# A fused transformer block on one core: fewer pair additions in five units, one transpose moved to TensorE, a new order, and the re-run test ahead of the last transfers

## The chip, the cores and the metric

The kernel runs on one core of one Trainium2 chip. The metric is device time in microseconds (us), the median of the runs of one kernel. The core's engines run side by side, each with its own instruction stream: TensorE (PE in the profile, its weight loads PEld), VectorE (DVE), ScalarE (ACT), GpSimd (POOL) and SyncE (SP), which in this kernel issues nearly all DMA transfers. Semaphores tie the streams together.

## The reference, cut to what matters

A transformer block over 2048 tokens of width 1024, with an attention half and a gated feed-forward half. Both halves are modulated by a vector `c`:

```python
sa, ca, ga, sb, cb, gb = split(silu(c) @ w_mod)
h = layernorm(x) * (1 + ca) + sa
q, k, v = h @ wq (32 heads of 32), h @ wk, h @ wv      # one k and one v for all heads
p = softmax(q k^T / sqrt(32));  x = x + ga * ((p v) @ wo)
h = layernorm(x) * (1 + cb) + sb
x = x + gb * ((silu(h @ w1) * (h @ w3)) @ w2)          # inner width 3584
```

Inputs and the output are bfloat16, the output 2048 x 1024.

## The kernel before, in words

Tokens are taken in 8 blocks of 256. For each block there are 8 attention units of 4 heads, so 64 units in all (`u`; block `u // 8`). A unit goes through the 2048 keys in 8 chunks, so there are 512 chunks. A chunk is eight score matmuls of 32 rows (`S<-QT,KT`, four side by side in the array), two exponentials on ACT (`U<-S`, 128x1024 each) into one of ten slots of `U`, and eight matmuls of the probabilities with V (`PB<-U,V`). The scores lie in six PSUM banks (`S` in the rows); two more (`PB`) serve everything else, and after the last chunk the six are used for that too.

The softmax denominators are made on two engines. VectorE adds the two key halves of two chunks at a time (`pairs`: `PS<-U`, 128x2048), then folds the eight results of a unit together with additions of 128x1024 (`PS<-PS`), and TensorE multiplies what is left with ones (`dens`: `PB<-PS,ONES`, four matmuls of 32 columns for each slot left). How far VectorE folds is `level(u)`: at 1 it doesn't fold and eight slots go to TensorE, at 2 four additions leave four slots, at 4 seven additions leave one. Before, units 0 to 7 are folded to level 2 (units 0 and 1 in a form of their own) and all later ones to level 4.

After a block's eight units come, in `wo` (from L1371), its output projection (`WO<-QT` rows), the residual, the second norm's statistics and its normalised tile `XNB`; then the norm is transposed and modulated, and the feed-forward half follows: 14 slabs of the products with w1 and w3 (`slab`; a tanh on ACT and two multiplications on VectorE each), and four quarters of the product with w2 (`quarter`, whose w2 slices come into `W2S`, and for the last block also into the memory of `QT` and `U`). The feed-forward half of a block is spread between the score chunks of the next block. What belongs to the last block runs after the last chunk.

The transpose of the second norm has two forms. Blocks 1 to 6 use two DMA transposes from `XNB` into the memory of the block before in `QT`, and eight modulations `QT<-QT,MODC` on VectorE. Blocks 0 and 7 use sixteen TensorE transposes (`IDENT,XNB`) into two PSUM banks, and VectorE modulates straight out of PSUM.

The program is recorded as a graph of operations (`Graph.op`). A table of numbers, `ORDER`, gives the sequence in which a small planner (`Placer`) commits them; that alone sets the order on each engine. A `b` behind a number picks the operation's other engine (`alts`): for the first norm's tiles and their copies ACT or VectorE, for the scaling of the first two columns of wq (`WO<-W,MODC`) VectorE or POOL. Where the planner's own clock sees TensorE idle for over 0.7 us in the middle of the run, `keep_on` puts in multiplications of the identity, `PB<-IDENT`, whose results are not used; `keep_warm` does so in the start (`S<-IDENT`).

The exponentials are taken without subtracting a maximum. A test at the end (`verdict`) writes a flag `AGAIN`; only if it is set does each engine run a second, guarded version of the whole program, which stands behind the first one in its stream. So each engine, at the end of its stream, waits for the flag, loads it (`TENSOR_LOAD`), and branches over the guarded program:

```python
for fn in self.ops[name]:
    fn(eng)
eng.wait_ge(sem[flag.sem], flag.val)
again = eng.value_load(tile)
with eng.If(again != 0):
    ... second.ops[name] ...
```

SyncE then waits for every output transfer, and a barrier of all engines ends the program. In the profile all recorded operations have line 22; the flag's load is L747, the branch L748, SyncE's waits L756, and the end of the block with its drains L758.

Of the kernel before, what the change touches and what calls it, by code (L numbers as in the profile page):

```python
# [119 lines left out]
7 1 11 0 4 2 5 8 3 6 16 12 9 13 10 17 18 60 22 15 19 59 20 27 14 21 28 412 29 37 30 31 23 24 26 32 36 77 33 38 61 39  # L120
69 40 34 102 41 25 62 35 68 63 42 70 103 64 71 65b 72 104 111 43 73 105 45 44 112 106 66 113 122 74 114 132 115 123
67 116 75 107 124 131 125 76 126 46 133 117b 47 127 108 134 128b 118 135 48 49 119 109 136 50 78 137 110b 129 79 80
130 162 99 81 82 163 85 58b 57 53 54 97 55 86b 52b 51 164 172 83 98b 56b 171 138 84 173 165 182 87 166 139 88 183 89
90 167 91 174 168 92 143 93 175 94 95 142 120 176 96 144 151 460 145 121b 140 146 152 461 169 153 147 141 462 154
148b 463 155 170b 464 149 156 184 192 242 185 150 186 177b 157b 465 187 466 243 421 191 158 467 178 193 159b 194 195
179 203 469 160 188b 196 470 197b 180 161 468 202 198 181 471 472 199b 189 473 204 211 100 205 206 190b 474 475 101
207 212 200 476 213 208b 222 214 223 201b 244 215 224 225 477 245 209 216 226 246 478 210 227 217b 228 229 247 230
480 232 248 233 234 231 235 479 249 218 236 250 252 219 251 481 253 487 254 482 255 237-239 256 240 483 501 241 484
# [5 lines left out]
317 316 585 318 591 609 319 610 592 320 594 611 595 321 612 596 613 593 597-599 587 600 614 601 615 605 602 616 603  # L134
282 604 283 617 606 618 607 284 619 608 285 633 327 620 621 328 286 622 329 634 330 623 332 331 624 635 333 625 334
335 626 636 627 322 336 628 323 637 324 629 630 325 631 638 337 338 326 632 339 656 340 657 287 341 288 658 639 659
289 660 290 640 641 661 642 291 662 643 663 644-648 664 665 652 649 650 666 342 680 343 667 668 651 344 669 653 345
# [9 lines left out]
1182 453 794 407 456 795 820 1308 454 455 408 796 1309 457 826 829-831 822 832 1310 1311 827 833 834 1312 835 836  # L147
409 840 1313 824 1314 410 828 1315 837 889 411 838 888 1316 1317 839 930 458 910 841 1318 842 909 844 843 846 847
931 1319 1320 845 459 848 1321 849 1332 851 1322 1323 850 852 1324 853 1334 854 1325 1326 855 867 1327 868 857 869
856 1328 870 858 1329 1337 859 862 1331 860 863 864 871 1330 865 861 1343 866 1357 1344 1358 873 1345-1347 872 1348  # L150
# [260 lines left out]
class Placer:  # L411

    SWITCH = {"F": 0.095, "S": 0.11, "A": 0.106, "C": 0.106}
    LAT = {("dve", "pe"): 0.12, ("act", "pe"): 0.1, ("act", "dve"): 0.06}
    SEM = 0.06
    SPAN = 8
    COLS = 12
    FULL = 36.0
    FETCH = 24.0
    GAP = 0.7  # L420

    def __init__(self, g, banks, later, plan, first=None, order=None):
        self.g = g
        self.plan = []
        off = {}
        for late, pes, sl, one, hold, change in plan:
# [312 lines left out]
    def emit_all(self, second, flag, tile, outs):  # L739
# [3 lines left out]
        def both(eng, name):  # L743
            for fn in self.ops[name]:
                fn(eng)
# [924 lines left out]
```

## Time and profile before

| | before |
|---|---|
| median of 3 runs | 1137.85 us (1137.28 to 1138.27) |
| profiled execution, its own time | 1138.92 us |
| its span, first to last instruction | 1137.1 us |
| PE busy | 1102.5 us (97%) |
| ACT busy | 1020.4 us (90%) |
| DVE busy | 993.3 us (87%) |
| POOL busy | 42.9 us (4%) |
| mean busy share of the DMA queue q1 | 66% |

The stages can be read from the views by their first and last instructions: the first exponential starts at 31.26 us, the last score chunk stands at 1031 us, and the last matmul ends at about 1131.7 us. A row of a group or of the timeline has start and length in us, then engine, line, operation, output and inputs by tile name without buffer numbers, shapes, and in brackets the idle time ahead of it and who ended it. PEclk in the windows is the granted TensorE clock as a share of full speed.

### The profile page before, as it was taken

Reading aid. Unit: us, or ns where it says so; the run is one execution under the profiler, and the core shown is the slowest. Engines: PE = TensorE matmul, PEld = TensorE weight load, DVE = VectorE, ACT = ScalarE, POOL = GpSimd, SP = SyncE. Lnnn points to the kernel's source line nnn. Section 1 sums busy time; section 2 is a strip of 40 time slices with the busy share of each in tenths; the row PEclk is TensorE's granted clock in tenths of the full one; section 3 lists DMA queues with packets and bytes.
Section 4 is the critical chain, followed back from the end, with each engine's and each line's share of the span. In section 5 each row is a group of like instructions: output and inputs, shape, how many; then the busy total and the mean of one; then the engine's idle time right before and its main releaser. Section 6 shows DMA issues by size and latency. Waiting matters only on the chain.

```text
span 1137.1 us, 37432 instructions
## 1 busy us (share of the span) xinstructions
PE 1102.5 (97%) x16864; PEld 755.2 (66%) x16891; DVE 993.3 (87%) x1634; ACT 1020.4 (90%) x1159; POOL 42.9 (4%) x93
## 2 busy tenths in 40 slices
PE   5999989999899999999999999999999999999998
PEld 5744546766467766777577766776667757777887
DVE  7998999999999989998999889998999899997441
ACT  5999999999999999999999999999999999993110
POOL 5300000000100000000000000000000000000000
PEclk9999999999999999999999999999999999999999
DMA  9321477675656676865696568768587558767983
GB/s 344 107 76 36 146 212 203 191 203 144 174 150 192 183 188 157 240 195 152 122 297 193 151 179 209 223 193 214 149 249 214 161 141 214 214 188 195 260 233 85
DMA packets 381544, 209.73 MB, mean 184 GB/s; under 512 B 17600, under 2 KB 373184, under 8 KB 381376
## 3 DMA queue, kind: packets, MB, share of 16 engines
q1 hardware_dynamic: 380944, 207.11, 66.0%
q8 instruction: 135, 2.21, 0.8%
q14 instruction: 33, 0.27, 0.1%
q10 hardware_dynamic: 432, 0.13, 0.1%
HBM read 199.89 MB, written 4.19 MB: 179 GB/s over the span
## 4 chain that ended last, share of the span: by engine, by line
PE 47%; ACT 41%; DVE 6%; DMA 2%; POOL 1%; issue 1%; SPq 1%; DVEq 0%
ACT U L22 38%; PE PB L22 34%; PE S L22 13%; ACT HT L22 3%; DVE PS L22 2%; DMA W<-in_A_wq_dram 1%; DVE ST L22 1%; DVE HT L22 1%; POOL RS L22 1%; SPq L22 1%; DMA HT<-in_B_w_dram 1%; DVE QT L22 1%; DMA W<-in_B_w_dram 0%; DVE X L22 0%; DVE XNB L22 0%
## 5 line engine op out<-in xcount | busy, mean ns | idle before, releaser
L22 ACT ACTIVATE U<-S 128x1024 bf16<-128x1024 f32 x1024 | 967.0, 1141 | 6.2 <-PE S L22 5.0
L22 DVE TENSOR_TENSOR PS<-U 128x2048 bf16<-128x2048 bf16 x256 | 308.8, 1213 | 9.6 <-ACT U L22 8.1
L22 DVE TENSOR_TENSOR PS<-PS 128x1024 bf16<-128x1024 bf16 (+1 forms) x420 | 284.5, 690 | 4.2
L22 PE MATMUL PB<-QT,W 128*128 128x256 bf16 (+1 forms) x2632 | 223.5, 273 | 0.1
L22 PE MATMUL S<-QT,KT 32*128 32x256 bf16 x4096 | 203.9, 273 | 7.9 <-ACT U L22 5.3
L22 PEld LDWEIGHTS PB<-QT,W 128*128 128x128 bf16 (+1 forms) x2632 | 167.4, 97 | 40.8 <-issue 22.2
L22 PE MATMUL PB<-W2S,HT 128*128 128x256 bf16 x1512 | 189.6, 273 | 0.0
L22 PEld LDWEIGHTS PB<-W2S,HT 128*128 128x128 bf16 x1512 | 137.1, 98 | 41.6 <-issue 22.6
L22 PEld LDWEIGHTS S<-QT,KT 32*128 32x128 bf16 x4096 | 60.8, 92 | 135.4 <-ACT U L22 121.8
L22 PE MATMUL PB<-U,V 128*32 128x256 bf16 x4032 | 126.9, 273 | 0.8 <-ACT U L22 0.8
L22 PE MATMUL PB<-QT,HT 128*128 128x256 bf16 (+1 forms) x1288 | 123.9, 273 | 0.9 <-DVE QT L22 0.6
L22 PEld LDWEIGHTS PB<-U,V 128*32 128x32 bf16 x4032 | 99.4, 96 | 23.2 <-issue 13.5
L22 ACT ACTIVATE HT<-PB 128x512 bf16<-128x512 f32 (+1 forms) x110 | 81.6, 741 | 32.0 <-PE PB L22 31.9
L22 PEld LDWEIGHTS PB<-QT,HT 128*128 128x128 bf16 (+1 forms) x1288 | 90.9, 97 | 23.2 <-issue 11.5
L22 PE MATMUL PB<-HT,W 128*32 128x512 bf16 (+2 forms) x884 | 97.8, 342 | 2.8 <-DVE HT L22 0.9
L22 DVE SCALAR_TENSOR_TENSOR HT<-HT,PB 128x512 bf16<-128x512 bf16 x103 | 70.4, 684 | 12.7 <-ACT HT L22 11.8
L22 PEld LDWEIGHTS PB<-HT,W 128*128 128x128 bf16 (+1 forms) x896 | 50.4, 97 | 33.2 <-issue 11.7
L22 DVE TENSOR_TENSOR HT<-HT,PB 128x512 bf16<-128x512 bf16 x98 | 66.7, 681 | 1.3 <-PE PB L22 0.6
L22 PE MATMUL PB<-WO,QT 128*128 128x512 bf16 (+1 forms) x266 | 54.8, 380 | 1.6 <-issue 1.3
L22 DVE STREAM_TRANSPOSE RB<-PB 128x256 f32<-128x256 f32 x63 | 28.1, 446 | 29.2 <-PE PB L22 28.7
L22 POOL TENSOR_SCALAR RS<-MV 128x1 f32<-128x1 f32 x32 | 13.4, 418 | 1001.0 <-DVE MV L22 994.8
L22 ACT ACTIVATE HT<-S 128x512 bf16<-128x512 f32 (+1 forms) x13 | 9.4, 728 | 36.7 <-PE S L22 36.7
(122 smaller groups left out, 674.8 us busy)
## 6 DMA issues: line engine op xcount, KB each, us to landing
W<-in_B_w_dram SPq DMA_DIRECT2D x150, 512.0 KB, 4.9
W2S<-in_B_w_dram SPq DMA_DIRECT2D x30, 1792.0 KB, 9.3
HT<-in_B_w_dram SPq DMA_DIRECT2D x74, 512.0 KB, 5.0
W2S<-in_w_mod_dram SPq DMA_DIRECT2D x8, 1024.0 KB, 5.7
X<-in_A_x_dram SPq DMA_DIRECT2D x8, 512.0 KB, 6.7
U<-in_w_mod_dram SPq DMA_DIRECT2D x4, 1024.0 KB, 11.6
out_dram<-X SPq DMA_DIRECT2D x7, 512.0 KB, 8.1
W2S<-in_A_x_dram SPq DMA_DIRECT2D x5, 512.0 KB, 11.1
```

Source lines behind the costliest of these rows:

```text
L22: return getattr(e, call[0])(*call[1], **call[2])
```

## The change

Four things change.

1. `level(u)` is 2 for units 13, 14, 15 and 17, and 1 for unit 16, which were all 4. That leaves out three additions in four units and seven in one, 19 of 128x1024, and adds 12 matmuls in four units and 28 in one, 76 of 32x256.
2. The second norm of block 1 takes TensorE's form of the transpose: two DMA transposes less, sixteen transposes of 128x128 more on TensorE; the eight modulations read PSUM.
3. `ORDER` is another sequence, from the first operation to the last.
4. In `both`, SyncE's last three operations and VectorE's last six are taken out of the main stream; the flag is tested ahead of them, and they are issued in both arms: ahead of the guarded program if the flag is set, and in a second `If` behind it otherwise. The other three engines keep their test at the end.

```diff
@@ ORDER (all lines differ; its first)
-7 1 11 0 4 2 5 8 3 6 16 12 9 13 10 17 18 60 22 15 19 59 20 27 14 21 28 412 29 37 30 31 23 24 26 32 36 77 33 38 61 39
+6 1 11 0 4 2 5 8 3 7 9 12 13 10 25 16-18 59 22 15 14 60 19 61 28 21 62 412 63 27 20 23 64 24 65 26 29 68 30 31 36 45
...
@@ class Placer
     GAP = 0.7
+    TAIL = {"sp": 3, "dve": 6}
...
         def both(eng, name):
-            for fn in self.ops[name]:
+            ops = self.ops[name]
+            cut = len(ops) - self.TAIL.get(name, 0)
+            for fn in ops[:cut]:
                 fn(eng)
             eng.wait_ge(sem[flag.sem], flag.val)
             again = eng.value_load(tile)
             with eng.If(again != 0):
+                for fn in ops[cut:]:
+                    fn(eng)
                 for s, v in last.items():
                     if v:
                         eng.wait_ge(sem[s], v)
                 for fn in second.ops[name]:
                     fn(eng)
+            if ops[cut:]:
+                with eng.If(again == 0):
+                    for fn in ops[cut:]:
+                        fn(eng)
             if name == "sp":
                 for n in outs:
                     eng.wait_ge(sem[n.sem], n.val)
...
         def level(u):
-            return 2 if u < 8 else 4
+            return {13: 2, 14: 2, 15: 2, 16: 1, 17: 2}.get(u, 2 if u < 8 else 4)
...
-                if 0 < n < NB - 1:
+                if 1 < n < NB - 1:
                     G.alias([("H2R", n, t)], h2k(n))
                     dma("sp", h2t(n)[:, :, t * P:(t + 1) * P], XN[t], ("H2", t), 1 << 18, reads=[("XN", t)],
                         writes=[("H2R", n, t)], vt=vt - 40, bw=100e3, transpose=True)
-            if 0 < n < NB - 1:
+            if 1 < n < NB - 1:
```

How the instructions stand is shown at three places. The first is the end of SyncE's stream. Before, the last output transfers, then the load of the flag and the branch; what stands behind the branch belongs to the guarded program:

```order
L22 DMA W2S<-in_B_w_dram 128x28x256
L22 DMA out_dram<-X 128x2x1024
L22 DMA out_dram<-X 128x2x256 x3
L22 DMA out_dram<-X 128x256 x2
L747 TENSOR_LOAD AGAIN
L748 COMPARE_AND_BRANCH
```

After, in the same place (the three rows behind the branch are those of the arm with the flag set, and stand once more behind the guarded program, after a second branch on line 760):

```order
L22 DMA W2S<-in_B_w_dram 128x28x256
L22 DMA out_dram<-X 128x2x1024
L22 DMA out_dram<-X 128x2x256 x2
L750 TENSOR_LOAD AGAIN
L751 COMPARE_AND_BRANCH
L22 DMA out_dram<-X 128x2x256
L22 DMA out_dram<-X 128x256 x2
```

Load and branch moved from behind the last transfer to between the transfers of the second and the third quarter. VectorE's stream has them in the corresponding place, ahead of its last three pairs of a multiplication and an addition.

The second place is TensorE around the second norm of block 1, from the end of that block's output projection (`WO<-QT`) to its first slab (`QT,HT` and `QT,W` are the norm times w1 or w3). Before:

```order
L22 MATMUL PB<-PS,ONES 32x256 x4
L22 MATMUL PB<-WO,QT 32x512 x8
L22 MATMUL S<-QT,KT 128x256 x16
L22 MATMUL PB<-IDENT 128x128 x12
L22 MATMUL S<-QT,KT 128x256 x8
L22 MATMUL PB<-IDENT 128x128 x12
L22 MATMUL S<-QT,KT 128x256 x8
L22 MATMUL PB<-U,V 32x256 x32
L22 MATMUL S<-QT,KT 128x256 x8
L22 MATMUL PB<-U,V 32x256 x32
L22 MATMUL S<-QT,KT 128x256 x8
L22 MATMUL PB<-IDENT 128x128 x12
```

After (the row ahead of the first is again the end of the projection):

```order
L22 MATMUL PB<-W2S,HT 128x256 x14
L22 MATMUL S<-QT,KT 128x256 x8
L22 MATMUL PB<-W2S,HT 128x256 x12
L22 MATMUL S<-QT,KT 128x256 x8
L22 MATMUL PB<-W2S,HT 128x256 x12
L22 MATMUL S<-QT,KT 128x256 x8
L22 MATMUL PB<-W2S,HT 128x256 x14
L22 MATMUL S<-QT,KT 128x256 x8
L22 MATMUL PB<-W2S,HT 128x256 x4
L22 MATMUL PB<-IDENT,XNB 128x128 x8
L22 MATMUL S<-QT,KT 128x256 x8
L22 MATMUL PB<-IDENT,XNB 128x128 x8
```

The 36 unused identity products are gone; a quarter of block 0's product with w2, 56 matmuls that stood ahead of the projection before, stands in the gap, and then the new transposes. In the whole stream the 46 `PB<-IDENT` of before (ten of them at block 0's second norm) are none, and the 92 `S<-IDENT` of the start are 85.

The third place is POOL in the start, where the first two columns of wq are scaled (`WO<-W,MODC`, eight operations shared with VectorE). Before:

```order
L22 TENSOR_SCALAR NB<-MV,RS 128x1
L22 COPY WO<-SAB 128x1024
L22 TENSOR_SCALAR WO<-W,MODC 128x256 x3
L22 TENSOR_SCALAR RS<-MV 128x1
L22 TENSOR_TENSOR RS<-RS,NH 128x1
```

After:

```order
L22 TENSOR_SCALAR NB<-MV,RS 128x1
L22 COPY WO<-SAB 128x1024
L22 TENSOR_SCALAR WO<-W,MODC 128x256 x2
L22 TENSOR_SCALAR RS<-MV 128x1
L22 TENSOR_TENSOR RS<-RS,NH 128x1
```

One of the eight moved from POOL to VectorE, which has six instead of five. The transfers that SyncE issues ahead of that part of wq are the same nine, in another sequence.

Over the stage between, the counts agree: 98 tanh operations stand ahead of the last exponential in both kernels. Behind the last score chunk TensorE has 812 matmuls of 128x256 before and 806 after, and the same number of every other kind.

More of the change, by code (lines that the diff above doesn't have):

```diff
@@ L119 @@
 ORDER = """
-7 1 11 0 4 2 5 8 3 6 16 12 9 13 10 17 18 60 22 15 19 59 20 27 14 21 28 412 29 37 30 31 23 24 26 32 36 77 33 38 61 39
[L121 to L124, printed above, removed]
@@ new lines @@
+4860 4872 4873 4815 4354 4816 4355 4874 4356 4817 4357 4358 4863 4359 4875 4876 4849 4360 4361 4877 4365 4406 4366
+4362 4367 4368 4878 4369 4846 4879 4370 4850 4880 4371 4372 4386 4893 4426 4387 4388 4373 4882 4881 4389 4374
+4390-4392 4894 4883 4393 4396 4847 4447 4397 4398 4394 4399 4885 4884 4400 4395 4401 4402 4848 4886 4403 4375 4448
+4376 4404 4377 4378 4887 4851 4888 4379 4380 4889 4852 4381-4383 4407 4427 4408 4890 4409 4916 4896 4861 4917
+4410-4412 4862 4413 4918 4414 4891 4919 4468 4902 4903 4415 4904 4905 4920 4864 4906 4416 4907 4908 4892 4909 4921
@@ new lines @@
+5073 4614-4618 5074 5075 5057 4619 5076 5058 4620 4621 5087 4622 4626 5077 4656 4627 5078 5089 4628 5079 4629-4632
+5080 4633 5060 4634 5061 5081 5062 4635 5082 4636 5090 4637-4639 5092 5083 4640 4641 5084 4642 5085 4643 5093 4644
+4645 4623 4646 5086 4647 5575 5088 4648 5576 4649 5094 4650-4653 5577 5578 4687 4654 5098 5099 5579 5100 5095
+5101-5103 4655 5580 5104 5096 5105 5581 5108 5582 4624 4657-4659 5091 4660 4661 5583 5097 5584 4662 4663 5585
+4664-4667 5586 5587 5106 4668 5588 5107 4669 4670 5601 4671 4672 5589 4673 5590 5599 4674 5591 4675-4679 5592 5109
@@ new lines @@
+6994 6981 7034 6995-6997 7014 6998 6982 6999-7001 6991 7015 7002 7055 7016-7019 7003 7020-7022 7004 7023 7076
+7005-7007 7024 7008-7011 7048 7012 7056 7036-7041 7049-7051 7025-7032 7052 7033 7077 7053 7042 7043 7098 7057 7044
+7058 7097 7059-7061 7045 7062-7064 7054 7078 7065 7118 7079-7082 7066 7083-7085 6422 7086 7139 7067-7070 7087
+7071-7074 6423 7075 7119 7088-7095 6424 7096 7140 7109-7116 7099-7106 7120 7107 7121-7124 7108 7125-7127 7117 7141
+7128 7142-7145 7129 7146-7148 6425 7149 7130-7133 7150 7134-7137 6426 7138 7151 7192 7152 7153 6427 7154-7157 6428
@@ L408 @@
+7158 6429 7159 7161-7190 7225-7231 7191 7193 7232-7252 7194 7253 7195-7198 7254 7199 7200 7255 7201-7222 7257-7263
+7223 7264-7270 7273 7271 7274-7276 7272 7277 7289 7278-7288 7290
 """
```

469 lines of the change are left out of this document (227 added, 242 removed), and 84 rows, old and new, of the table ORDER.

## The prediction

> **What bounds the kernel now.** I read the windows first, cut at the first exponential, the last score chunk and the last matmul. (Columns: each engine's busy us in the window and its instructions; then granted clock, DMA share, GB/s.)
>
> ```profile
> core 0: us, PE busy (x) PEld busy (x) DVE busy (x) ACT busy (x) POOL busy (x), PEclk, DMA share, GB/s
> ...
> 31.00:1033.00 1002.00, 985.22 (x15670) 655.31 (x15692) 925.83 (x1497) 995.00 (x1128) 24.90 (x46) 1.00 0.65 178
> 1033.00:1132.00 99.00, 97.70 (x915) 83.40 (x915) 43.44 (x80) 8.96 (x15) 1.76 (x4) 1.00 0.78 207
> 1132.00:1138.00 6.00, 0.00 (x0) 0.00 (x0) 0.47 (x2) 0.00 (x0) 0.00 (x0) 0.76 0.07 19
> ```
>
> Ahead of these lies a start of 31 us. Then each stage has its own limit: 1002 us in which ACT is busy for 995 and PE for 985; 99 us of PE almost alone; and 6 us in which no engine but VectorE computes, for 0.5. What the change is worth must be read in each by itself. VectorE, which gets the largest relief, has 76 us to spare in the long stage.
>
> The long stage's limit is ACT, so I next asked what ACT waited for in the stretch of the changed units, 138 to 320 us (the total wait, how often, the longest):
>
> ```profile
> ACT U L22 <- PE S L22: 1.3, 4, 0.6
> ACT HT L22 <- PE PB L22: 0.5, 2, 0.3
> ```
>
> ACT stands idle for 1.8 us there, always for PE. PE idles more, at block 1's second norm:
>
> ```profile
> 306.00:317.00 11.00, 7.21 (x152) 4.52 (x153) 10.13 (x23) 11.00 (x14) 1.72 (x2) 1.00 0.25 69
> ...
> L22 PE MATMUL PB<-IDENT 128*128 128x128 bf16 x36 | 2.5, 220 | 0.0
> ```
>
> Of 11 us PE is busy 7.2, and 2.5 of that are the unused identity products; so 6.3 us do no useful work until the transposed norm arrives. But ACT's entry for the same window is 11.00: it didn't notice. PE time freed there is worth something only where PE is the limit, which is in the 99 us behind the last chunk.
>
> Last, the final 6 us. Behind VectorE's last addition the streams read:
>
> ```profile
> 1132.21 0.29 DVE L22 TENSOR_TENSOR X<-X,HT 128x256 bf16<-128x256 bf16 x1
> ...
> 1132.53 0.34 SPq L22 DMA_DIRECT2D out_dram<-X  x1
> ...
> out_dram<-X SPq DMA_DIRECT2D x1, 64.0 KB, 1.6
> ...
> L747 SPq TENSOR_LOAD <-AGAIN x1: 505/505/505, 1132.9 to 1132.9; - x1
> L748 POOLq COMPARE_BRANCH  x1: 45/45/45, 1052.6 to 1052.6; - x1
> L748 PEldq COMPARE_BRANCH  x1: 3622/3622/3622, 1130.2 to 1130.2; - x1
> L748 DVEq COMPARE_BRANCH  x1: 72/72/72, 1132.8 to 1132.8; - x1
> L748 SPq COMPARE_BRANCH  x1: 53/53/53, 1133.5 to 1133.5; - x1
> L756 SPq EVENT_SEMAPHORE  x6: 17/28/28, 1136.3 to 1136.7; - x6
> L758 POOLq DRAIN  x1: 107/107/107, 1053.1 to 1053.1; - x1
> L758 PEldq DRAIN  x1: 73/73/73, 1133.8 to 1133.8; - x1
> L758 DVEq DRAIN  x1: 58/58/58, 1135.8 to 1135.8; - x1
> L758 SPq COMPARE_BRANCH  x1: 43/43/43, 1136.7 to 1136.7; - x1
> L758 SPq DRAIN  x1: 13/13/13, 1136.9 to 1136.9; - x1
> ```
>
> The last transfer is issued at 1132.5 and lands 1.6 later, at 1134.1. SP meanwhile loads the flag (0.5), branches at 1133.5 and shows nothing until its first wait at 1136.3: 2.8 us in which no wait holds it. Two others show the same between branch and drain, VectorE 2.9 and PE 3.6, but POOL, whose guarded program is short, 0.5. So the long jump costs 2.8 to 3.6 us, and SP's jump, not the landing, ends the program: all waits pass at once, then 0.5 us to the end at 1137.1.
>
> **The change part by part.** The sum is made against the profiled execution, 1138.92 us, which is its span of 1137.1 and 1.8 around it; it lies 1.1 above the median.
>
> *The branch ahead of the last transfers.* SP's load and jump now stand behind the second quarter's transfer. What is queued behind them is the third quarter's transfer, and on VectorE the third quarter's multiplication, for which the rows give the slack:
>
> ```profile
> 1120.25 0.42 DVE L22 TENSOR_TENSOR X<-X,HT 128x512 bf16<-128x512 bf16 x1
> 1125.64 0.69 DVE L22 TENSOR_TENSOR HT<-S,GBR 128x512 bf16<-128x512 f32 x1 [4.96 <-PE S L22]
> ```
>
> VectorE's load (0.5) and jump (2.9) begin at about 1120.3 and end near 1123.8, 1.8 us ahead of its next input; with PE's 3.6 still 1.1 ahead. SP would be back by about 1124.6 and is wanted at 1126.8. At the end SP then waits for the landing at 1134.1 instead of its jump; with the 0.2 from its branch to its drain and 0.2 for the barrier the span ends near 1134.5. VectorE drains at about 1132.7. PE's jump stays where it is and drains at 1133.8, 0.5 ahead of SP: that is what is late next. Gain 1137.1 - 1134.5 = 2.6. Bounds: 0.5, if the closing jump of the new arm cost SP another 2.8 behind its last issue; 2.6 at most, since the landing holds. I take 2.6: SP's branch at 1136.7 to code right behind it cost 0.2.
>
> *The start.* The first exponential hangs on wq's first columns and POOL's three scalings of them:
>
> ```profile
> 24.71 2.94 POOL WO L22 x3
> 24.65 1.29 DVE L22 TENSOR_SCALAR WO<-W,MODC 128x256 bf16<-128x256 bf16 x5 [0.42 <-DMA W<-in_A_wq_dram]
> 26.37 0.71 PE L22 MATMUL PB<-IDENT,XNB 128*128 128x128 bf16 x8
> 27.79 1.03 PE L22 MATMUL PB<-HT,WO 128*128 128x256 bf16 x8 [0.71 <-POOL WO L22]
> 31.26 2.84 ACT L22 ACTIVATE U<-S 128x1024 bf16<-128x1024 f32 x3
> ```
>
> Two scalings end 0.98 earlier; VectorE's six end at 26.2, earlier still. PE's own transposes run to 27.1, so the products start 0.7 earlier, and the chain to 31.26 with them. Nine transfers stand ahead of wq as before, so 24.7 stays. The first norm's last tile is fetched later, behind the rest of wq and one chunk of the modulation weights; bound for that is a loss of 1, the other end a gain of 1. I take 0.7.
>
> *Fewer additions, a TensorE transpose, and the norm's gap.*
>
> ```profile
> L22 DVE TENSOR_TENSOR PS<-PS 128x1024 bf16<-128x1024 bf16 x416 | 279.6, 684 | 4.2
> ...
> 147.68 0.62 PE L22 MATMUL PB<-PS,ONES 128*32 128x256 bf16 x16
> 304.07 0.29 PE L22 MATMUL PB<-PS,ONES 128*32 128x256 bf16 x4
> 174.67 1.07 PE L22 MATMUL PB<-IDENT,XNB 128*128 128x128 bf16 x16 [0.72 <-DVE XNB L22]
> ```
>
> VectorE: 19 x 0.684 = 13.0 off. It isn't the limit, so by itself this is worth nothing, and that the eight modulations now read PSUM costs nothing either; the 76 us to spare hide both. What it does is to bring the norm's chain forward. PE: 76 matmuls at (0.62 - 0.29)/12 = 0.0275 are 2.1, and the transposes 1.1: 3.2 on, within the 6.3 us which the quoted window loses. If that cover were gone, ACT would wait for scores up to 3.2. The two DMA transposes leave SP's queue, and the transfers behind them are issued earlier; this I count at nothing, since ACT waited for no transfer. The gap itself: 56 matmuls of block 0's product with w2, at 0.109 (below) 6.1 us, stand in it now, so PE loses almost nothing there. What ACT gets of it is at most its 1.8 of idle time, at least a loss: the new transposes stand in PE's queue ahead of a score chunk, and if `XNB` is late, as at block 0 by 0.72, the scores behind it are late too; two halves, so up to 1.4. I take half of 1.8, 0.9.
>
> *The new order behind the last chunk.*
>
> ```profile
> 1113.21 6.28 PE L22 MATMUL S<-QT,HT 128*128 128x256 bf16 x56
> ...
> 1060.00:1070.00 10.00, 9.31 (x86) 8.10 (x85) 3.34 (x5) 1.20 (x2) 0.00 (x0) 1.00 0.97 261
> ```
>
> Fifty-six matmuls take 6.28 with the last one's 0.17 of latency: 0.109 each. Six fewer, 812 to 806, are 0.65. But PE lost 0.7 of the 10 us quoted while the DMA engines were 0.97 busy with weights: what PE gains it may have to wait for. Between 0 and 0.65 I take 0.3. In the stretch between block 2 and the last chunk I count neither gain nor loss: the kinds and numbers are the same, ACT is full. Its bounds are an estimate from the 1.8 us that 182 us of the changed stretch held: either way about 1.5.
>
> Sum: -2.6 - 0.7 - 0.9 - 0.3 = -4.5. From 1138.92 to 1134.4, and from the median 1137.85 to 1133.4 (0.4% less; a measurement of this kernel tells 0.2%, 2.3 us, from no change).
>
> **The rivals.**
>
> *The end doesn't move.* The arm with the transfers closes with a jump of its own, and if that is fetched like a long one, SP ends at 1132.9 + 2.8 and its waits: 0.5 won instead of 2.6, in all 1135.5. For it: the three long jumps cost 2.8 or more. Against it: POOL's 0.5 and SP's 0.2 over short distances. [...]
>
> *PE's clock falls where the identity products went.* This row is from the start, where PE's work had been thin:
>
> ```profile
> 35.00:40.00 5.00, 5.00 (x56) 3.60 (x53) 3.93 (x10) 4.71 (x7) 1.52 (x4) 0.66 0.64 213
> ```
>
> One fall took 0.34 of 5 us, 1.7 us of PE's time, in which ACT went on with 4.71 of 5. The two norms had 46 products as a cover and the clock stayed at 1.00. If it now falls at both, PE owes 3.4 us and ACT, from its 0.29 idle, waits some 0.6: 1134.0, within my range. [...]
>
> *The searched order misjudges the last stage: slower.* In the window 1060 to 1070 the weights arrive no faster than they are used. A w2 slice is 1.79 MB, 6.9 us at the 261 GB/s of the row above. If one now stands ahead of a slab half that PE needs, PE stalls for that: 1133.4 + 6.9 = 1140.3. It decides from 4.5 us of new stalls on. Against it: SP's queue has the same number of slab halves between the same w2 slices in both kernels.
>
> *More is won in the long stage.* If all of ACT's 1.8 goes, and as much in later blocks by the 1.5 above, 1131.0.
>
> **How the numbers follow.** Forecast as summed 0.56; more won 0.13; the end doesn't move 0.12; clock falls 0.05; slower order 0.14. Predicted 1133.4. The range goes up past the second case by the start's lower bound of a loss of 1 and the rest, to 1136.8, and down to the larger win, 1131.0; most of the slower case, and a little at either end, is left out. Faster by over 0.2% (under 1135.6): the forecast, the larger win, the clock case, and half of the second case, less a tail of the first: 0.76; same 0.10; slower 0.14.
>
> **What would show it.** In the profile after: SP's load and branch near 1120 and its last wait, not a jump, ahead of the end; less than 2 us between the last `out_dram` issue and the drain. The first exponential at about 30.5. At block 1's norm `W2S` matmuls instead of identity products, ACT full. PE's tail from the last chunk about 98 to 98.5 long. Wrong I would be if the clock is below 1.00 near 170 or 305 us, if PE shows new waits on `W` or `HT` transfers behind 1033, or if VectorE reaches the third quarter late.

## The result

The kernel after takes 1134.65 us (median; 1134.0 to 1135.81), the kernel before beside it 1138.27 (1137.28 to 1140.32): a ratio of 0.9966, 95% interval 0.9956 to 0.9975. That is 3.6 us or 0.3% less; forecast were 4.5. The profiled execution's span went from 1137.1 to 1132.8. The windows of the profile after, cut as before at the first exponential, the last score chunk and the last matmul (same columns):

```profile
31.00:1032.00 1001.00, 988.12 (x15449) 654.50 (x15448) 917.90 (x1479) 994.85 (x1128) 24.42 (x46) 1.00 0.65 178
1032.00:1130.00 98.00, 96.89 (x910) 82.77 (x908) 41.57 (x77) 8.88 (x15) 1.76 (x4) 1.00 0.78 208
1130.00:1134.00 4.00, 0.00 (x0) 0.00 (x0) 0.70 (x2) 0.00 (x0) 0.00 (x0) 0.88 0.08 20
```

The long stage is one us shorter, the stage of PE alone one, and the last piece, in which nothing computes, went from 5.1 us to 2.8. The streams at the end of the kernel after (the flag's load is now L750, the branch L751, the jump past the second copy of the last operations L760, SP's waits L765, the end of the block L767):

```profile
1130.45 0.29 DVE L22 TENSOR_TENSOR X<-X,HT 128x256 bf16<-128x256 bf16 x1
...
L750 DVEq TENSOR_LOAD <-AGAIN x1: 544/544/544, 1118.7 to 1118.7; - x1
L750 SPq TENSOR_LOAD <-AGAIN x1: 485/485/485, 1119.6 to 1119.6; - x1
...
L751 DVEq COMPARE_BRANCH  x1: 72/72/72, 1119.3 to 1119.3; - x1
L751 SPq COMPARE_BRANCH  x1: 58/58/58, 1120.1 to 1120.1; - x1
L751 PEldq COMPARE_BRANCH  x1: 3707/3707/3707, 1128.4 to 1128.4; - x1
...
L760 DVEq COMPARE_BRANCH  x1: 50/50/50, 1122.3 to 1122.3; - x1
L760 SPq COMPARE_BRANCH  x1: 40/40/40, 1122.8 to 1122.8; - x1
...
L765 SPq EVENT_SEMAPHORE  x6: 17/28/28, 1131.2 to 1132.3; - x6
...
L767 DVEq DRAIN  x1: 330/330/330, 1130.5 to 1130.5; - x1
L767 PEldq DRAIN  x1: 72/72/72, 1132.2 to 1132.2; - x1
L767 SPq COMPARE_BRANCH  x1: 38/38/38, 1132.4 to 1132.4; - x1
L767 SPq DRAIN  x1: 13/13/13, 1132.6 to 1132.6; - x1
```

SP and VectorE branch near 1120 and are back at 1122.8 and 1122.3: the jump still takes 2.6 and 2.9 us, but VectorE's next input came at 1123.9. SP's last wait, at 1132.3, now ends with the landing of the last transfer, and PE's late jump drains 0.4 ahead of SP. From the start of the last matmul to the end it was 5.69 us; it is 3.13.

ACT's waits between 138 and 320 us, and the window of block 1's second norm, after:

```profile
ACT HT L22 <- PE PB L22: 0.5, 2, 0.3
...
ACT U L22 <- PE S L22: 0.4, 2, 0.2
```

```profile
306.00:317.00 11.00, 8.73 (x217) 5.77 (x215) 9.75 (x19) 11.00 (x14) 0.00 (x0) 1.00 0.78 218
...
304.58 1.70 PE L22 MATMUL PB<-W2S,HT 128*128 128x256 bf16 x14
306.21 0.40 PE L22 MATMUL S<-QT,KT 32*128 32x256 bf16 x8
306.54 0.61 PE L22 MATMUL PB<-W2S,HT 128*128 128x256 bf16 x4
306.99 0.61 PE L22 MATMUL PB<-IDENT,XNB 128*128 128x128 bf16 x8
```

ACT's 1.8 us of waiting became 0.9; the product with w2 stands where the identity products stood, and ACT is full there, as it was before.

Where the time went can be followed by the starts of the exponentials. The table is made from them in the profiled executions (us from the span's start; the column of the last matmul has its start too; a star marks a stretch in which PE's clock fell, which is told below):

```
                              chunk 0     16      48      80      96     160     208     496     511  last matmul   end
before                          31.26   66.23* 125.25  187.10  219.62  342.88  436.02 1001.76 1031.59   1131.44  1137.13
after                           30.95   65.00  124.32  184.65  217.61  340.75  433.98  999.93 1030.57   1129.68  1132.81
before, branch ahead            31.09   65.07  124.10  187.06* 219.59  343.22* 436.37 1002.24 1032.07   1131.60  1134.74
after, branch not ahead         31.03   65.08  124.39  185.98* 218.93  342.12  435.33 1001.38 1032.02   1130.39  1136.07
after, a second time            31.11   66.15* 125.46  185.79  218.75  341.95  435.07 1001.03 1031.67   1130.81  1133.97
```

Of the pair's 4.3 us the end has 2.56. Of the other 1.8, 1.2 stand already at chunk 16, ahead of every edited unit, and between chunks 160 and 496 nothing is added: the lead goes from 2.1 to 1.8.

### The profile page after: what moved, and what is told of

It reads as the page before. It is cut to its first block, busy times and chain, and to the rows that moved or that the text cites. A ratio compares the mean times of both kernels' runs of the same rounds, so it can differ in the third digit from the quotient of the medians.

```text
span 1132.8 us, 36935 instructions
## 1 busy us (share of the span) xinstructions
PE 1104.8 (98%) x16642; PEld 754.1 (67%) x16642; DVE 983.7 (87%) x1615; ACT 1021.8 (90%) x1160; POOL 41.0 (4%) x92
## 4 chain that ended last, share of the span: by engine, by line
ACT 46%; PE 43%; DVE 6%; DMA 3%; issue 1%; SPq 1%; POOL 0%; DVEq 0%
ACT U L22 44%; PE PB L22 31%; PE S L22 13%; ACT HT L22 3%; DVE PS L22 2%; DMA W<-in_A_wq_dram 1%; DVE ST L22 1%; DMA W2S<-in_B_w_dram 1%; DVE HT L22 1%; SPq L22 1%; DMA W<-in_B_w_dram 1%; DVE X L22 0%; POOL RS L22 0%; DVE QT L22 0%; DVE RB L22 0%
## 5 line engine op out<-in xcount | busy, mean ns | idle before, releaser
L22 DVE TENSOR_TENSOR PS<-PS 128x1024 bf16<-128x1024 bf16 (+1 forms) x401 | 272.4, 690 | 4.2
L22 PE MATMUL PB<-QT,W 128*128 128x256 bf16 (+1 forms) x2448 | 228.4, 273 | 0.6 <-DVE QT L22 0.5
L22 PE MATMUL PB<-QT,HT 128*128 128x256 bf16 (+1 forms) x1248 | 116.5, 273 | 1.2 <-issue 1.1
L22 PEld LDWEIGHTS PB<-QT,HT 128*128 128x128 bf16 (+1 forms) x1248 | 85.1, 97 | 22.0 <-issue 11.7
L22 DVE SCALAR_TENSOR_TENSOR HT<-HT,PB 128x512 bf16<-128x512 bf16 x99 | 67.6, 683 | 7.4 <-ACT HT L22 6.3
L22 ACT ACTIVATE HT<-S 128x512 bf16<-128x512 f32 (+1 forms) x17 | 11.8, 696 | 61.6 <-PE S L22 61.6
L22 PE MATMUL PB<-WO,QT 128*128 128x512 bf16 x224 | 55.7, 381 | 0.0
```

Of the source, the lines that this page charges most:

```text
L22: return getattr(e, call[0])(*call[1], **call[2])
```

## The experiments

They ran in three groups, four rows of the table each. In each group the ratio is to the kernel before on the same chip, beside it; its medians there were 1139.01, 1139.13 and 1138.72 us. The second group was on another chip than the other two.

| kernel | median us | ratio to before, 95% |
|---|---|---|
| before, branch ahead | 1136.59 | 0.9984 (0.9975 to 0.9992) |
| after, branch not ahead | 1137.49 | 0.9989 (0.9980 to 0.9998) |
| after, branch ahead on SP alone | 1136.25 | 0.9983 (0.9973 to 0.9993) |
| all edits, old order | 1143.33 | 1.0036 (1.0022 to 1.0050) |
| after, additions back | 1139.84 | 1.0008 (0.9998 to 1.0018) |
| after, q bias copied early | 1136.33 | 0.9972 (0.9960 to 0.9984) |
| before, branch ahead, padded | 1144.58 | 1.0047 (1.0031 to 1.0063) |
| after, padded | 1140.05 | 1.0008 (0.9999 to 1.0017) |
| after, a second time | 1135.02 | 0.9970 (0.9959 to 0.9981) |
| after, start by the norm | 1136.46 | 0.9982 (0.9972 to 0.9991) |
| old order, branch, TensorE transposes | 1140.04 | 1.0011 (1.0002 to 1.0020) |
| old order, branch, fewer additions | 1138.87 | 0.9998 (0.9988 to 1.0007) |

### The end: who jumps, and when

```diff
  # the kernel before
+ TAIL = {"sp": 3, "dve": 6}      # and both() of the kernel after
```

> The kernel before with one edit: SP's and VectorE's test of the flag stands ahead of their last 3 and 6 operations, as in the kernel after; order, additions and transposes as before. Theory (the long jump of SP, and with it VectorE's, ended the program, and nothing else of the change touches the end): 2.6 us less than before, so about 1135.7 where before is 1138.3; SP's last wait ends some 1.6 us behind its last issue instead of 4.1, and the drain follows within 0.5. Rival (the end of the kernel after is short because its new order brings the last transfers in differently): 0 to 0.5 less, 1137.8 or more.

```diff
  # the kernel after
- TAIL = {"sp": 3, "dve": 6}
+ TAIL = {}
```

> The kernel after with the test of the flag back behind all of SP's and VectorE's operations. Theory: 2.6 us more than after, so about 1137.2 where after is 1134.65, and 1.0 to 1.8 less than before, which is what the rest of the change is worth. Rival (the rest of the change is worth nothing by itself): equal to before within 0.3.

```diff
  # the kernel after
- TAIL = {"sp": 3, "dve": 6}
+ TAIL = {"sp": 3}
```

> The kernel after with the test ahead of the last operations on SP alone; VectorE tests behind its last addition. Theory (a long jump costs each engine 2.5 to 3.7, and the end waits for the last engine): VectorE's last addition at 1130.5, load 0.5, jump 2.9, so it drains near 1133.9, behind SP's last wait at 1132.4; the end comes 1.3 to 1.6 later than in the kernel after, about 1136.1. Rival (only SP's jump ends the program, VectorE's lies beside the transfer): equal to after within 0.3.

By medians the branch alone won 2.4 us in the old order, and the rest of the change 1.5 without it (their intervals, 0.9 to 2.8 and 0.2 to 2.3, contain 2.6 and 1.0 to 1.8). The traces are sharper than the medians: from the start of the last matmul to the end it is 5.69 in before, 5.68 in the kernel without the branch ahead, 3.13 in after and in before with the branch ahead, whatever the order. With SP alone it is 4.62, and the streams say why. The branch, SP's waits and the drains of that kernel:

```profile
L751 SPq COMPARE_BRANCH  x1: 58/58/58, 1119.8 to 1119.8; - x1
L751 PEldq COMPARE_BRANCH  x1: 3707/3707/3707, 1128.1 to 1128.1; - x1
L751 DVEq COMPARE_BRANCH  x1: 72/72/72, 1130.7 to 1130.7; - x1
...
L765 SPq EVENT_SEMAPHORE  x6: 17/28/28, 1130.9 to 1132.1; - x6
...
L767 SPq DRAIN  x1: 13/13/13, 1132.3 to 1132.3; - x1
L767 DVEq DRAIN  x1: 59/59/59, 1133.7 to 1133.7; - x1
```

SP is done at 1132.3; VectorE jumps at 1130.7, is back 2.9 later, and the end waits for it: 1.5 us, as expected. So in these traces the jump costs SP 2.6 to 2.8 us and VectorE 2.9 wherever it stands, and PE 3.6 to 3.7 at the end of its stream, and the program ends with the last engine to have jumped or with the landing. The theory of the first and the third experiment holds, and their rivals fall. The rival of the second, equal to before within 0.3, lies just inside the interval of 0.2 to 2.3 and isn't excluded.

### The edits and the order: neither does without the other

The order of the kernel before was put on the program after, with each new operation where the old one stood:

```diff
- ORDER = the kernel after's
+ ORDER = the kernel before's; the sums of units 16 and 17 ahead of the additions that overwrite their inputs,
+         block 1's two groups of transposes each ahead of its modulations
```

> The kernel after, with all its edits, in the order of the kernel before (the two products that sum the denominators of units 16 and 17 had to move ahead of the additions that now overwrite their inputs; block 1's two groups of transposes stand where its modulations stood). Theory (the 1.8 us won ahead of the last matmul come from the new order, above all in the first 66 us, where 1.2 of them already stand; the edits on VectorE and the norm are worth nothing): the branch's 2.6 alone, about 1135.7 where before is 1138.3, with chunk 16 where it was before. Rival (the edits win 0.9 or more at block 1's norm by themselves): 1134.8 or less.

It is not 2.6 us better than before but 4.3 worse, 6.7 above the same order without the edits. Neither expectation held. So the edits were put into the old order one at a time:

```diff
  # the kernel before with the branch ahead
- if 0 < n < NB - 1:      # DMA transposes for block 1 too
+ if 1 < n < NB - 1:      # TensorE transposes for block 1
```

> The first experiment (the kernel before with the branch ahead of the last transfers) with one more edit: block 1's second norm transposed by TensorE, where its modulations stood; all additions kept. Theory (PE's second group of transposes waits for a bank that VectorE's modulations empty late, and a score chunk stands behind it; this is what cost the old order with all edits its 5 us): as that kernel, 3 to 6 us above the first experiment, with ACT waiting 3 us or more between 315 and 335. Rival (it was the fewer additions, whose sums PE must make early): equal to the first experiment within 0.7.

```diff
  # the kernel before with the branch ahead
- return 2 if u < 8 else 4
+ return {13: 2, 14: 2, 15: 2, 16: 1, 17: 2}.get(u, 2 if u < 8 else 4)
```

> The first experiment with the other edit: units 13 to 17 with 19 additions fewer, their sums made by PE, block 1's norm by DMA as before. Theory (VectorE's time is no limit in the old order, and PE's 28 us-hundredths per product are hidden): equal to the first experiment within 0.7. Rival (the sums' early place is what hurt): 2 us or more slower, with ACT waiting for scores between 270 and 320.

Against the old order with the branch alone (1136.59) the transposes cost 3.5 us and the fewer additions 2.3. Some of the 3.5 goes with a lower clock, of which more is said below: executions at the same mean granted clock differ by 2.0 (at 0.995) and 2.6 (at 0.994, where the one kernel has a single execution), and for the fewer additions by 2.4 (0.997). The first theory's wait is there. PE, and then ACT, in the old order with the transposes:

```profile
314.32 0.62 PE L22 MATMUL PB<-IDENT,XNB 128*128 128x128 bf16 x8
316.67 1.02 PE L22 MATMUL PB<-IDENT,XNB 128*128 128x128 bf16 x8 [1.74 <-DVE QT L22]
317.63 0.61 PE L22 MATMUL S<-QT,KT 32*128 32x256 bf16 x8
319.24 2.72 PE L22 MATMUL PB<-QT,HT 128*128 128x256 bf16 x12 [1.00 <-DVE QT L22]
```

```profile
318.29 1.94 ACT L22 ACTIVATE U<-S 128x1024 bf16<-128x1024 f32 x2 [1.61 <-PE S L22]
322.56 1.02 ACT L22 ACTIVATE U<-S 128x1024 bf16<-128x1024 f32 x1 [2.33 <-PE S L22]
```

The second group of transposes waits 1.74 us for `QT`, VectorE's modulations of the first; the score chunk stands behind it in PE's stream, and ACT waits 1.6 and then 2.3. In this trace the clock is also at 0.50 from 316.72 to 323.55, so that eight transposes take 1.02 instead of 0.62; the wait and the fall can't be parted here. And only this placing was tried, with no score chunk between the two groups; in the kernel after one stands there, and the second group, at 308.24, doesn't wait.

The fewer additions cost without one great wait: from chunk 112 to 160 that trace needs 93.2 us where the old order with the branch needs 91.5. The loss is spread over five units, 0.2 to 1.0 us each. My theory for them, equal within 0.7, fell. What fits is PE: in the old order it was busy for 33.95 of the 34 us from 252 to 286 already, and the added products with ones are 2.1 us by the forecast's own price. The new order has room for them, for it moved products with w2 out of that stretch into the norm's gap (223 of them between 252 and 300 us in the old order, 165 in the new). That this is the cause is argued, not shown by a run.

The reverse, the additions put back into the new order:

```diff
  # the kernel after
- return {13: 2, 14: 2, 15: 2, 16: 1, 17: 2}.get(u, 2 if u < 8 else 4)
+ return 2 if u < 8 else 4
  # ORDER: each of the 19 additions right behind the operation that makes its second input
```

> The kernel after with the 19 additions of units 13 to 17 put back, each right behind the operation that makes its second input, everything else in the order of the kernel after. Theory (VectorE is no limit anywhere in that stretch; fewer additions are worth nothing by themselves): as the kernel after within 0.5 us, ACT at 904 ns per exponential between 180 and 320 us as before. Rival (block 1's norm chain needs the 13.0 us of VectorE's time): the norm comes later, PE's score chunks with it, and ACT loses 0.9 us or more between 290 and 330 us.

It is 4.8 us slower than the kernel after run in the next group (4.4, each against the kernel before beside it). VectorE, PE and ACT of that kernel at block 1's product with wo:

```profile
290.11 1.22 DVE L22 TENSOR_TENSOR PS<-U 128x2048 bf16<-128x2048 bf16 x1
291.36 1.42 DVE L22 TENSOR_TENSOR PS<-PS 128x1024 bf16<-128x1024 bf16 x2
292.70 1.28 DVE L22 TENSOR_TENSOR X<-X,PB 128x512 bf16<-128x512 bf16 x2
```

```profile
291.30 0.40 PE L22 MATMUL S<-QT,KT 32*128 32x256 bf16 x8
293.43 1.47 PE L22 MATMUL PB<-WO,QT 128*128 128x512 bf16 x6 [1.74 <-DVE X L22]
...
303.70 3.17 PE L22 MATMUL PB<-W2S,HT 128*128 128x256 bf16 x14 [1.23 <-DVE X L22]
```

```profile
295.28 9.27 ACT L22 ACTIVATE U<-S 128x1024 bf16<-128x1024 f32 x10 [1.38 <-PE S L22]
307.28 9.27 ACT L22 ACTIVATE U<-S 128x1024 bf16<-128x1024 f32 x10 [2.72 <-PE S L22]
```

In the kernel after, the residual additions `X<-X,PB` that empty PE's banks start at 289.17. Here a pair and two of the added additions stand ahead of them, they start at 292.70, PE waits 1.74 for the bank, the scores behind it are late, and ACT waits 1.4 and 2.7. The last row shown of PE has a fall of the clock in it, from 303.48: its 14 products take 3.17 us, where they took 1.70 in the kernel after. The 4.8 us aren't this fall's, though: five executions of this kernel with a mean clock of 0.999, where this one has 0.997, average 1139.9, no less than its median of 1139.84. VectorE, with 83 us to spare in the long stage of the kernel after, is the limit in these 20 us. The rival is right in kind and its 0.9 too small. The additions were put in one place only; a better one may exist.

### PE's clock

A clock that falls shows in many of the traces. The kernel after, a second time (windows of one us):

> The kernel after itself, beside the three that follow and the kernel before on one chip. In the runs so far executions of the kernel before are slower the lower their mean granted clock (1136.7 at 0.999, about 1137.8 at 0.998, 1140.4 at 0.993); the kernel with all of the change but the branch has the same times at equal clocks (1137.9 at 0.998) and higher clocks on the whole. Theory: the kernel after has a clock of 0.998 to 1.000 and lies 2.5 us below before at equal clock, 3.3 to 3.9 below its median. Rival (the order and the edits are worth 1 us or more by themselves): 3.5 us or more below before at equal clock.

```profile
34.00:35.00 1.00, 1.00 (x47) 1.00 (x44) 1.00 (x3) 1.00 (x2) 0.87 (x2) 1.00 0.17 63
35.00:36.00 1.00, 1.00 (x18) 0.98 (x15) 1.00 (x3) 0.91 (x1) 0.69 (x2) 0.71 0.14 26
36.00:37.00 1.00, 1.00 (x13) 0.78 (x14) 0.96 (x4) 0.93 (x1) 0.41 (x1) 0.50 0.74 229
37.00:38.00 1.00, 1.00 (x12) 0.44 (x5) 1.00 (x2) 0.61 (x2) 0.82 (x3) 0.50 1.07 380
38.00:39.00 1.00, 1.00 (x6) 0.57 (x4) 0.67 (x2) 1.00 (x2) 0.03 (x1) 0.58 1.04 364
39.00:40.00 1.00, 1.00 (x16) 0.69 (x15) 0.85 (x2) 0.93 (x2) 0.00 (x0) 1.00 0.20 66
```

The granted clock goes to 0.50 at 35.4 and back 3.41 us later (the rows lack 1.71 us of clock, as they do in before, whose fall begins at 35.98), with PE's busy entry full all along. The same program's first trace had no fall here: its chunk 16 came at 65.00 us, this one's at 66.15. Falls stand at 35 to 36, 145 to 154 and 303 to 320 us (one at 965); each lasts 3.41 us or twice that, and where one trace has several they lie whole multiples of 3.41 apart (46 of them between 153.58 and 310.60 in before with the branch ahead). What they cost: 1.0 us at the start (the two traces of after, by the stretch from the first exponential to chunk 16), 0.1 to 1.3 at block 0's norm (chunks 48 to 80 in the new order: 60.7, 61.0 and 61.6 with a fall, 60.3 to 60.6 without), 0.4 at block 1's (chunks 144 to 160: 32.65 against 32.26).

What brings them? PE's busy time in the profile doesn't sort them: by it the 3.41 us ahead of a fall are busy for 0.36 to 0.99, and stretches of 0.52 to 0.65 have no fall behind them. So I cut each trace into stretches of 3.41 us, at whole multiples from where its clock changes, and for each summed rows x columns x streamed columns over the matmuls, as a share of 32 products of 128 x 128 with 256 columns (at 0.109 us, the usual spacing of such products in the traces, 31 fit). In the 14 traces there are 18 falls between 30 and 1034 us, all behind a stretch of 0.16 to 0.365; once fallen, the clock stayed down over stretches of 0.33 to 0.376 and rose behind 0.375 and more. Against it: two traces have no fall behind 0.32 to 0.34 at 120 and 137 us. Every other stretch at full clock used 0.376 or more. In the trace of before the one ahead of the fall used 0.365 and no other under 0.378; the 3.41 us from 150.2 on used 0.13, but they lie across two stretches, and no fall follows. A score chunk, with 32 of 128 rows, counts as two such products, 0.22 us at their spacing, of some 1.8 between chunks. Small products stand side by side in the array (eight of 32 rows take 0.40 us in the rows above, eight of 128 rows 1.05 in those of the start below), so the measure nearly equals the share of time in which any product streams its columns (0.20 to 0.39 ahead of the falls, at 0.109 for 256 columns); which of the two counts isn't shown.

So, it seems, one program has more or fewer falls by the accident of where these stretches begin, and its time varies with the clock. Executions of the kernel before beside these experiments, grouped by mean granted clock, and the kernel after without the branch ahead, whose end is equally long:

```
clock     before: executions, mean us       after, branch not ahead
0.993        10   1140.5
0.994        21   1139.5
0.995        10   1139.8
0.996         7   1139.2
0.997        17   1138.3                       4   1137.4
0.998        14   1137.8                       6   1138.0
0.999         3   1137.3
1.000         2   1136.0                       1   1136.3
all          84   1138.9  (clock 0.9958)      11   1137.6  (clock 0.9978)
```

At equal clock the two differ by -0.9 to +0.3 us; over all executions by 1.3. The slope of the left column is 0.5 us per 0.001, so the higher clock would account for about 1.0 of the 1.3. This is a correlation: a wait that slows an execution also thins PE's work and may bring a fall, and no run parts the two. Against so high a price stand the first seven executions of the kernel after: four at 1.000 average 1134.8, three at 0.998 average 1134.9. That the new order has fewer falls agrees with the traces: counting for which beginnings of the stretches the use would be 0.365 or less gives, as an estimate, 2.0 to 2.6 falls for the two traces of the old order (before, and with the branch ahead) and 1.2 to 1.5 for four of the new (1.8 with the bias copied early). What remains of the order and the edits together is, by this, some tenths, not the 1 us of the rival. The kernel after, this second time, had 0.998 in every execution and a mean of 1135.5, 2.3 below the left column there, near the theory's 2.5. The mean clock also counts a fall behind the last matmul, which the longer end holds more of (in the trace of before 0.52 over the last 2.13 us), so this last comparison is a rough one.

Can the falls be bought off? Products of the identity ahead of score chunks raise the use:

```diff
+ PAD = {chunk: products}     # 2-5: 5, 43-46: 5, 52-55: 5, 57-66: 8, 72-76: 5, 140-149: 6
+ # ahead of chunk c, in the score buffer that ACT freed earlier: PAD[c] unused 128x128x128 products
```

> The first of these experiments (the kernel before with only the branch ahead of the last transfers) with 5 to 8 products of the identity matrix with itself ahead of each score chunk at the thin places (chunks 2 to 5, 43 to 46, 52 to 55, 57 to 66, 72 to 76, 140 to 149), in a score buffer that is free. In the traces so far PE's clock fell to 0.50 for 3.41 us behind each 3.41 us in which the matmuls used 0.365 of the array or less (rows x columns x streamed columns against 128 x 128 at full clock), and never behind 0.375 or more; that is how the count of products was chosen. Theory (the old order loses some 2 to 3 such falls in an execution, about 0.9 us each, and the new order is faster ahead of the last matmul only because it has fewer): clock 0.999 to 1.000, 1.5 to 2.2 us less than without the products, so near 1134.7 where before is 1139.0. Rival (the order itself is worth 1.2 to 1.8, the clock nothing): 1136.6 or more, since the products only take PE's time.

```diff
+ PAD = {chunk: products}     # on the kernel after; 2-5: 5, 43-46: 4, 52-55: 4, 57-66: 6, 72-76: 4
```

> The kernel after with 4 to 6 such products ahead of the score chunks 2 to 5, 43 to 46, 52 to 55, 57 to 66 and 72 to 76. Theory: the new order's traces give about 1.2 falls an execution; without them clock 1.000 and about 1 us less than the kernel after, 1133.5 where before is 1138.3 to 1139. Rival (its falls cost nothing, since ACT's stream is full around them): as the kernel after, or slower by the products' own time, up to 0.5.

The mean clock rose to 0.999 and more in both, and both lost: 8.0 and about 5 us. In the kernel after chunks 48 to 64 need 29.2 us, padded 32.7, for 58 products, which at their spacing of 0.055 are 3.2 by themselves. So where the array is thinly used PE's stream has no time to spare either: the products go on the path whole, and a fall of 1.3 us at most is cheaper than its cure. My theory on the price fell with it; that the falls are the old order's whole loss can't be read from these two.

### The start

```diff
  # VectorE, the kernel after
  WO<-W,MODC x6
+ QBI<-PB
  MV<-ST
  ST<-W2S x2
- QBI<-PB
```

> The kernel after, with VectorE's copy of the q bias (27.27 in the trace) put ahead of the two statistics that it stands behind, and its 16 products on PE with it. Theory (the first products of q wait for the PSUM bank that this copy empties, not for the scalings): the products begin when PE's transposes end, near 26.65 instead of 27.46, and the first exponential comes 0.6 to 0.8 earlier, near 30.2; of this the end gets the same if ACT limits all the way, and nothing if PE's work behind the last chunk gives it back. Rival (they wait for ACT's copy of the transposes at 26.7 to 27.7, or for another scaling): no change of the first exponential.

The first products of q in the kernel after, and ACT's stream to the first exponential:

```profile
27.46 1.05 PE L22 MATMUL PB<-HT,WO 128*128 128x256 bf16 x8 [0.84 <-POOL RS L22]
...
27.27 0.14 DVE L22 COPY QBI<-PB 128x2 f32<-128x2 f32 x1
...
29.17 1.24 ACT L22 ACTIVATE XNB<-W2S,NB,RS 128x1024 bf16<-128x1024 bf16 x1 [1.48 <-POOL NB L22]
30.57 0.47 ACT L22 ACTIVATE KT<-PB,KBI 128x256 bf16<-128x256 f32 x1 [0.17 <-PE PB L22]
30.95 2.84 ACT L22 ACTIVATE U<-S 128x1024 bf16<-128x1024 f32 x3
```

With the copy at 26.08 the products begin at 26.68, as the theory has it: the bank was the wait. But the first exponential came at 30.78, only 0.2 earlier, and the end no earlier at all: on ACT it stands behind a normalisation that starts at 29.23 there, 29.17 in after and 29.01 in before, waiting for GpSimd. That was taken away next:

```diff
  # VectorE and GpSimd: tile 10's statistics and chain ahead of tile 11's; QBI and the two copies of q early
  # PE
+ MATMUL S<-QT,KT x8          # the first score chunk
  MATMUL PB<-HT,WO x8         # a product for k
- MATMUL S<-QT,KT x8
```

> The kernel after, with tile 10's statistics ahead of tile 11's on VectorE and GpSimd, the q bias copied early, the two copies of q ahead of the statistics beside them, and the first score chunk ahead of one product for k. Theory (in the kernels before and after and with the early copy ACT's normalisation of tile 10 starts at 29.01, 29.17 and 29.23, waiting for GpSimd, and the first exponential stands behind it on ACT; this is the limit of the start): the normalisation starts near 27.9, the first exponential near 29.4 to 29.8, 1.2 to 1.5 earlier than in the kernel after; the end follows by 0.8 to 1.2 where ACT is the limit. Rival (PE's products limit the start): the first exponential at 30.3 or later; or the end gives it back, and the time is that of the kernel after.

The normalisation starts at 27.91 and the first exponential at 29.27, 1.7 ahead of the kernel after. None of it arrives: chunk 16 starts at 65.43, 0.4 later than there, and the median is 1.4 above (the intervals of the two ratios overlap). PE and ACT of this kernel:

```profile
33.52 0.71 PE L22 MATMUL PB<-IDENT,WO 128*128 128x128 bf16 x8 [1.63 <-DVE WO L22]
...
31.94 1.02 ACT L22 ACTIVATE U<-S 128x1024 bf16<-128x1024 f32 x1 [0.32 <-PE S L22]
34.26 1.02 ACT L22 ACTIVATE HT<-PB 128x1024 bf16<-128x1024 bf16 x1 [1.30 <-PE PB L22]
```

PE waits 1.63 for VectorE at 33.5, and ACT gives 1.6 back at once. In the other kernels whose clock didn't fall there, with either order, chunk 16 starts at 64.9 to 65.1 (padded ones aside), with first exponentials between 30.88 and 31.09. The engine that is full on the way to chunk 16 is VectorE, in this kernel busy for 33.4 of the 34 us from 31 to 65 where ACT is busy for 32.0. So the stretch is set by VectorE and not by the first exponential; this rests on the one way of moving it that was tried. No kernel here beats the kernel after.

## Why the prediction came out as it did

The time was forecast at 1133.4 (1131.0 to 1136.8) and is 1134.65. By its steps:

- **The end, 2.6: right**, 2.56 in the trace, by the mechanism forecast, with VectorE's jump as necessary as SP's. The rival with the closing jump fell: behind L760 both engines go on with what they were given, and behind L767 SP drains in 0.2.
- **The start, 0.7: wrong.** The failed step is "the products start 0.7 earlier, and the chain to 31.26 with them". The products started 0.33 earlier, for they waited for a PSUM bank which VectorE emptied behind two statistics. The first exponential moved 0.31 in this pair, but most of that is scatter: other traces of the old order have it at 30.98 to 31.09, others of the new with the same start at 30.84 to 31.11 (padded ones aside). And moving it by 1.7 was worth nothing at chunk 16. The 1.2 us by which the profiled after leads there are a fall of the clock in the profiled before.
- **The norm, 0.9: the size of ACT's gain right, its cause wrong.** ACT's 1.8 us became 0.9. But 0.77 of that lies between 138 and 180 us, at block 0's norm, which no edit but the order touches: ACT's busy time there went from 40.81 to 41.58, and 19.68 to 19.86 at block 1's. The new order did it: without a fall in either, chunks 48 to 80 take 60.3 us against 61.9, and 0.4 of this is given back by chunk 96. From chunk 16 to the last matmul, where neither trace of the pair has a fall, 0.5 is left of it. The failed step is "it isn't the limit, so by itself this is worth nothing": alone, fewer additions cost 2.3 us in the old order, and putting them back costs 4.8 in the new one. "3.2 on, within the 6.3 us which the quoted window loses" held in the kernel after, where ACT stays full at block 1's norm, but it doesn't follow from the idle time: most of the products with ones lie ahead of that window, and the transposes cost 3.5 in the old order. A stretch's idle time says nothing of who stands behind a waiting matmul.
- **The order behind the last chunk, 0.3: not shown.** From the last score chunk PE needs 99.5 instead of 100.3, but the last 15 chunks are 0.8 longer; from chunk 496 on it is 129.7 in both. In the other traces of the new order with all edits and no padding it is 128.5 to 129.8, in the old one with the branch 129.4.
- **The middle, 0: right.** Chunks 208 to 496 take 565.7 and 566.0.
- **The clock: its falls foreseen, their sign wrong.** I had falls as a rival by which the new kernel would lose. They are no new thing but in both kernels, and the new order has fewer. This term, about 1 us by the slope above and 1.0 in the profiled pair's start, is missing from the sum, and it stands where the start and the norm were to be. That the time still came within 1.3 us of the forecast is, for this part, luck.

The slower rival, a w2 slice ahead of a slab half that PE needs, didn't come: PE is busy 96.89 of the 98 us behind the last chunk. (Its price was a little low: a slice of 128x28x256 bfloat16 numbers is 1.84 MB, 7.0 us at 261 GB/s.) That more is won in the long stage didn't come either.

What stays open: how much of the gain ahead of the last matmul is the clock's and how the rest, some tenths, divides among the places; and why the clock didn't fall at 120 and 137 us in two traces.

## What to carry to other kernels

A conditional jump over a long program at the end of every stream was a cost of its own here (2.6 to 3.7 us on SP, VectorE and PE), and moving each late engine's jump into an earlier wait took it off the path; with one engine left out the end waited for it, 1.5 us. An edit that relieves an engine with slack on average was worth 5 us in one order and cost 2 to 3 in the other, according to what stands behind it in another engine's stream, so edit and order are to be tried together as well as apart. Before explaining a microsecond between two traces, look whether PE's clock fell in one of them.

## What the runs showed of the hardware

PE's clock fell to 0.50 for 3.41 us or twice that, also where the profile calls PE busy, behind stretches that used 0.16 to 0.365 by rows, columns and streamed columns (two such stretches, at 0.32 to 0.34, had no fall behind them), at places that shift from one execution to the next. The branch over the guarded program took SP 2.6 to 2.8 us and VectorE 2.9, hidden or not, and PE 3.6 to 3.7; between branch and drain ACT shows 4.2 in before and 2.5 in after; POOL, whose guarded program is short, shows 0.5, and SP's branch at the end of the block 0.2.
